# GFNet mixing and ReGLU on one core: last stores in multiples of 16 rows, the first input in four parts, slab loads queued behind the last slab store, and a longer lag in the first inverse transform

## The chip, the cores and the metric

The kernel runs on one core of a Trainium2 chip. The metric is the device time of one execution in microseconds (us), as the median of several executions. Executions that lie more than 1.5% above the fastest of the same kernel would be set aside as slow. A profile is one execution recorded by the hardware profiler. Its span is about 2 us shorter than the device time (967.1 against 969.6 us before), because the device time includes a little that lies outside the recorded span.

The engines are PE (matrix multiply), ACT (ScalarE), DVE (VectorE), POOL (GpSimd) and SP (used here only to issue DMAs). SP, ACT and POOL each have an in-order instruction stream, and each can issue DMAs from it. In a timeline, "SPq" or "ACTq" marks a stretch in which that stream was issuing DMAs.

## The reference

```python
# x: [8, 3008, 256], filters: [1505, 256], w_gate and w_val: [256, 1536], w_out: [1536, 256]
X = np.fft.rfft(x, axis=1)
y = np.fft.irfft(X * (filt_r + 1j * filt_i)[None], n=3008, axis=1)
t = y.reshape(24064, 256)
out = (np.maximum(t @ w_gate, 0.0) * (t @ w_val)) @ w_out
```

The kernel computes the Fourier transforms as matrix products over 3008 = 94 x 32. Stage A multiplies by a 94-point table (`psA`), stage B does the 32-point part, the filter and its inverse (`psX`, then `tt` and `uu`, then `psD`), and stage C finishes the inverse (`psY`). The feed-forward part then works on 47 blocks of 512 tokens (`psV`, `psG`, `psO`). Batches 1 to 7 of the transform are slipped in between the blocks. Only batch 0 has to be transformed before the first block can start, and only the last block's output has to be stored after the last matmul. These two ends are all that the change touches.

## The kernel before

Batch 0 goes through this chain: x from HBM into `XF`; 16 items of stage A, each a matmul into `psA` and a copy on ACT into `asb`; after every fourth item a store of `asb` to `Abuf` (a "slab store"); four "slab loads" of `Abuf` into `at`, in another layout; stage B; and so on. Stage B cannot start before all four slabs are in `at`.

```python
def load_at(b, c):                     # one slab: 32 x 24 runs of 512 bytes
    nc.sync.dma_start(ats[b][c:c + 125:4], _ap(Abuf[b], c * NROW * NC2 * D, [[D, 32], [4 * NC2 * D, NG], [1, D]]))

# in items_a, item j of slab c (cut)
nc.tensor.matmul(psA[0:NROW], WA[:, :NROW], XF[...][:, o:o + 512], start=True, stop=True)
nc.scalar.copy(dst, psA[0:NROW])
if j == 3:
    nc.sync.dma_start(_ap(Abuf[b], ...), st["asb"])

# in items_b: fwd(g) makes psX, tt (DVE) and uu (DVE, or for six g of batch 0 GpSimd) and appends to `held`;
# inv() takes the oldest of `held`, makes psD from tt and uu, copies it to dsb
for g in range(0, NG, 2):
    def both(g=g):
        fwd(g)
        if amid:
            amid(g // 2)
        if len(held) > 2:              # the lag
            inv()
    yield both
yield inv
yield inv

# the start (cut)
load_x(0, nc.sync, ((0, 0, 2 * q), (0, 2 * q, 4 * q), WHOLE[1]))
nc.sync.dma_start(tabs, ...)           # tables
hold_gpsimd(XF[0][:, 4 * q - 8:])      # GpSimd issues the filter loads only when this part of x is there
load_filters()
for i, f in enumerate(items_a(0)):
    f()
    if 9 <= i < 15:
        make_back(0, i - 9)            # psI: inverse tables, made from F2
    else:
        warm(1, 256)
    if i % 4 == 3 and i > 3:
        load_at(0, i // 4 - 1)
load_at(0, 3)
...
nc.sync.dma_start(gate, ats[0][0:32, NG - 1, 0:8])   # reads `at`: makes SP wait for the slabs
load_x(1, nc.sync, WHOLE)                            # x of batch 1
def amid(i):                           # inside stage B of batch 0:
    if i < 9:
        warm(1, 128)
    else:
        next(early)()                  # from the tenth step on, stage A of batch 1
```

The output is stored as follows. `runs` cuts 128 tokens into runs of at most 94 rows of 1 KB each, which lie 32 rows apart in the output.

```python
# in o_part; t is the quarter of the block, last the last block (cut)
nc.scalar.copy(osb[:, t0 % 2:t % 2 + 1], psO[:, t0 % 2:t % 2 + 1])
for tt in range(t0, t + 1):
    for i, (o, b, n2, n1, w) in enumerate(runs(blk * W + tt * 128, 128)):
        eng = nc.sync
        if last:
            eng = nc.gpsimd if t in (1, 2) else (nc.sync, nc.scalar)[i % 2]
        eng.dma_start(_ap(out, (b * S + n1 * N2 + n2) * D, [[N2 * D, w], [1, D]]), osb[o:o + w, tt % 2])
```

## Time and profile before

The median was 969.61 us (969.28 to 969.72 in 3 runs). Marks read from the trace split the span of 967.1 us into three parts:

| part | from, to (us) | length (us) |
|---|---|---|
| start: to the first psV matmul | 0, 60.83 | 60.83 |
| middle: first psV matmul to the end of the last matmul | 60.83, 958.10 | 897.28 |
| tail: from there to the span's end | 958.10, 967.1 | 8.96 |

The page of the kernel before gives each engine's busy time with its share of the span and its instruction count, and the shares of the chain of waits that ended last. PE is the bound, and only the two ends leave it idle for long.

```profile
PE 940.9 (97%) x5926; PEld 564.1 (58%) x6036; DVE 546.5 (57%) x823; ACT 527.4 (55%) x945; POOL 45.2 (5%) x81
...
PE 93%; DVE 2%; ACT 1%; issue 1%; DMA 1%; POOL 1%; SPq 0%; POOLq 0%; DVEq 0%; ACTq 0%
```

The stretches view of the tail before has these columns: the stretch and its length, then busy time and instruction count of PE, PEld, DVE, ACT and POOL, then the granted PE clock, the DMA engines' busy share and GB/s. From 962 us on, no compute engine has anything left, and the DMA engines are 12% and then 6% busy. Of 16 engines, 12% is two and 6% is one.

```profile
958.00:960.00 2.00, 0.10 (x1) 0.00 (x0) 0.00 (x0) 0.37 (x1) 0.76 (x2) 1.00 0.38 93
960.00:962.00 2.00, 0.00 (x0) 0.00 (x0) 0.00 (x0) 0.00 (x0) 0.00 (x0) 0.89 0.34 109
962.00:964.00 2.00, 0.00 (x0) 0.00 (x0) 0.00 (x0) 0.00 (x0) 0.00 (x0) 0.50 0.12 43
964.00:966.00 2.00, 0.00 (x0) 0.00 (x0) 0.00 (x0) 0.00 (x0) 0.00 (x0) 0.50 0.06 19
```

The timeline of ACT in the tail before gives start, length, engine, line, operation and count, and in brackets the idle time before it and what ended that. The last copies run at 956.83 and 958.14, right behind PE, and the last store is issued at 958.54. The landing records of that 94-row store show it complete at 965.62.

```profile
954.61 0.60 ACTq L406 DMA_DIRECT2D out_dram<-osb  x1
955.52 0.37 ACT L400 COPY osb<-psO 128x256 f32<-128x256 f32 x1 [0.94 <-PE psO L395]
956.83 0.37 ACT L400 COPY osb<-psO 128x256 f32<-128x256 f32 x1 [0.94 <-PE psO L395]
958.14 0.37 ACT L400 COPY osb<-psO 128x256 f32<-128x256 f32 x1 [0.94 <-DMA out_dram<-osb]
958.54 0.25 ACTq L406 DMA_DIRECT2D out_dram<-osb  x1
```

In the start, these are three of the waits of PE before 62 us (what waited, for what, us in total, times, the longest). The 4.4 us before psX are labelled "issue", but they end with the last slab load: the SP timeline below shows the read of `at` by `gate` passing at 35.02, and psX starts at 35.05.

```profile
PE psX L295 <- issue: 4.4, 1, 4.4
...
PE psD L315 <- POOL uu L302: 1.9, 4, 0.7
PE psI L189 <- DVE F L179: 1.0, 1, 1.0
```

The timeline of SP in the start before shows slab stores (`Abuf<-asb`) and slab loads (`at<-Abuf`) taking turns. A load waits for the landing of its own slab's store, and the last store, issued at 26.03, landed at 31.1.

```profile
21.59 0.31 SPq L268 DMA_DIRECT2D Abuf<-asb  x1
22.62 0.60 SPq L282 DMA_DIRECT2D at<-Abuf  x1
26.03 0.30 SPq L268 DMA_DIRECT2D Abuf<-asb  x1
28.16 3.56 SPq L282 DMA_DIRECT2D at<-Abuf  x2
35.02 0.31 SPq L459 DMA_DIRECT2D gate<-at  x1
```

### The profile page before, as it was taken

What the parts mean: (1) busy time and instruction counts of PE and PEld (TensorE: products, weight loads), DVE (VectorE), ACT (ScalarE), POOL (GpSimd) and SP (SyncE); (2) the same over time, 40 slices, a digit from 0 to 9 for tenths busy, and PEclk for the clock granted to TensorE, in tenths of its full rate; (3) what the DMA queues carried; (4) which work ended last, traced back from release to release, by engine and by line L of the source; (5) the groups of instructions that cost most, each with busy time, mean ns of one, the idle gap of its engine ahead of it and who ended that gap; (6) DMA issues with size and microseconds to landing.
All of it is one profiled execution on the core that took longest, in us unless ns stands there. A gap on an engine that the chain in (4) does not pass through costs nothing.

```text
span 967.1 us, 16199 instructions
## 1 busy us (share of the span) xinstructions
PE 940.9 (97%) x5926; PEld 564.1 (58%) x6036; DVE 546.5 (57%) x823; ACT 527.4 (55%) x945; POOL 45.2 (5%) x81
## 2 busy tenths in 40 slices
PE   8799999999999999999999999999999999999996
PEld 3446665466654666556665566655666556666664
DVE  3737855368543785437754377534775348655552
ACT  3665555555555555555555555555555555555552
POOL 4311000010000100001000010000100000000001
PEclk9899999999999999999999999999999999999998
DMA  9898151362523524135242352523524231241111
GB/s 248 247 242 250 61 127 30 101 209 65 119 57 83 205 81 112 49 101 191 77 115 55 104 197 55 115 70 109 174 64 113 69 110 41 82 99 34 33 33 45
DMA packets 94070, 105.64 MB, mean 109 GB/s; under 512 B 7724, under 2 KB 84929, under 8 KB 92298
## 3 DMA queue, kind: packets, MB, share of 16 engines
q1 hardware_dynamic: 87374, 81.44, 30.6%
q0 software_dynamic: 6432, 22.98, 8.1%
q8 instruction: 47, 0.77, 0.3%
q14 instruction: 33, 0.27, 0.1%
q10 hardware_dynamic: 184, 0.18, 0.1%
HBM read 58.67 MB, written 49.81 MB: 112 GB/s over the span
## 4 chain that ended last, share of the span: by engine, by line
PE 93%; DVE 2%; ACT 1%; issue 1%; DMA 1%; POOL 1%; SPq 0%; POOLq 0%; DVEq 0%; ACTq 0%
PE psO L395 25%; PE psG L376 25%; PE psV L376 23%; PE psA L263 10%; PE psY L360 2%; PE psD L315 2%; PE psX L295 2%; PE psD L314 2%; DMA tabs<-dft_tab 1%; DVE prod L381 1%; ACT vsb L379 1%; PE psJ L416 0%; POOL uu L302 0%; SPq L166 0%; ACT Fti L227 0%
## 5 line engine op out<-in xcount | busy, mean ns | idle before, releaser
L381 DVE SCALAR_TENSOR_TENSOR prod<-psG,vsb 128x512 bf16<-128x512 f32 x564 | 389.6, 691 | 368.0 <-ACT vsb L379 358.6
L379 ACT CAST vsb<-psV 128x512 bf16<-128x512 f32 x564 | 331.2, 587 | 212.1 <-PE psV L376 118.8
L395 PE MATMUL psO<-WoT,prod 128*128 128x256 bf16 x2256 | 336.5, 273 | 1.3
L376 PE MATMUL psG<-yT,WgT 128*128 128x512 bf16 x1096 | 328.5, 379 | 3.7
L376 PE MATMUL psV<-yT,WvT 128*128 128x512 bf16 x1051 | 319.2, 379 | 1.5 <-ACT yT L365 0.4
L395 PEld LDWEIGHTS <-prod 128*128 128x128 bf16 x2256 | 220.7, 98 | 143.4
L376 PEld LDWEIGHTS <-WgT 128*128 128x128 bf16 x1128 | 110.0, 98 | 134.0 <-issue 0.8
L376 PEld LDWEIGHTS <-WvT 128*128 128x128 bf16 x1128 | 104.2, 98 | 59.6 <-issue 49.5
L266 ACT CAST asb<-psA 96x512 bf16<-96x512 f32 x128 | 74.4, 581 | 109.3 <-PE psA L263 106.9
L263 PE MATMUL psA<-XF,WA 128*96 128x512 f32 x256 | 130.0, 593 | 0.9 <-DMA XF<-in_x_dram 0.9
L317 ACT CAST dsb<-psD 128x512 bf16<-128x512 f32 x96 | 56.2, 586 | 52.6 <-PE psD L315 50.6
L400 ACT COPY osb<-psO 128x512 f32<-128x512 f32 (+1 forms) x96 | 55.3, 577 | 29.3 <-PE psO L395 26.9
L298 DVE TENSOR_TENSOR tt<-psX,Ftr 128x512 bf16<-128x512 f32 x96 | 65.3, 681 | 4.5 <-PE psX L295 4.5
L304 DVE TENSOR_TENSOR uu<-psX,Fti 128x512 bf16<-128x512 f32 x90 | 61.2, 680 | 0.0
L315 PE MATMUL psD<-uu,I2u 128*128 128x256 bf16 x192 | 47.6, 275 | 1.9 <-POOL uu L302 1.9
L314 PE MATMUL psD<-tt,I2t 128*128 128x256 bf16 x192 | 48.1, 277 | 0.0
L360 PEld LDWEIGHTS <-dC 96*128 96x128 bf16 x604 | 34.6, 97 | 13.3 <-issue 10.8
L367 DVE CAST yT<-psY 128x512 bf16<-128x512 f32 x47 | 32.1, 683 | 17.5 <-PE psY L360 17.5
L295 PE MATMUL psX<-at,F 128*128 128x256 bf16 x192 | 37.6, 280 | 4.4 <-issue 4.4
L263 PEld LDWEIGHTS psA<-XF,WA 128*96 128x96 f32 x256 | 34.9, 163 | 8.8 <-ACT asb L266 3.6
L365 ACT CAST yT<-psY 128x512 bf16<-128x512 f32 x47 | 27.5, 585 | 19.6 <-PE psY L360 19.5
L360 PE MATMUL psY<-M,dC 96*128 96x94 bf16 (+18 forms) x604 | 37.7, 199 | 0.0
(52 smaller groups left out, 161.5 us busy)
## 6 DMA issues: line engine op xcount, KB each, us to landing
XF<-in_x_dram POOLq DMA_DIRECT2D x34, 512.0 KB, 6.6
Abuf<-asb SPq DMA_DIRECT2D x32, 384.0 KB
at<-Abuf SPq DMA_DIRECT2D x32, 384.0 KB
dC<-Dbuf SPq DMA_DIRECT2D x64, 192.0 KB
Dbuf<-dsb SPq DMA_DIRECT2D x31, 384.0 KB
out_dram<-osb SPq DMA_DIRECT2D x70, 94.0 KB
XF<-in_x_dram SPq DMA_DIRECT2D x9, 512.0 KB
XF<-in_x_dram SPq DMA_DIRECT2D x6, 256.0 KB
```

The costliest lines, as they stand in the source:

```text
L263: nc.tensor.matmul(psA[0:NROW], WA[:, :NROW], XF[c * NC2 // NX2][:, o:o + 512], start=True, stop=True)
L266: nc.scalar.copy(dst, psA[0:NROW])
L295: nc.tensor.matmul(psX[:, i], F2[:, g + i, :], at[:, g + i, :], start=True, stop=True)
L298: nc.vector.tensor_tensor(tt, psX, Ftr[:, g:g + 2, :], op=ALU.mult)
L304: nc.vector.tensor_tensor(uu, psX, Fti[:, g:g + 2, :], op=ALU.mult)
L314: nc.tensor.matmul(psD[:, i], I2t[:, g + i, :], tt[:, i], start=True, stop=False)
L315: nc.tensor.matmul(psD[:, i], I2u[:, g + i, :], uu[:, i], start=False, stop=True)
L360: nc.tensor.matmul(psY[:, o:o + w], dCs[b, n2 // 4][:, n2 % 4, h * 128:(h + 1) * 128], M1[:, n1:n1 + w], start=True, stop=True)
L376: nc.tensor.matmul(pt[:, :W], w[:, h, ft * 128:(ft + 1) * 128], yt[:, h, :], start=(h == 0), stop=(h == 1))
L379: nc.scalar.copy(vsb, psV[:, :W])
L381: nc.vector.scalar_tensor_tensor(prod, in0=psG[:, :W], scalar=0.0, in1=vsb, op0=ALU.max, op1=ALU.mult)
L395: nc.tensor.matmul(psO[:, t % 2], prods[ft][:, t * 128:(t + 1) * 128], WoT[:, ft, :], start=(ft == 0), stop=(ft == NFT - 1))
```

## The change

It has four parts:

1. The last block's stores are cut into a multiple of 16 rows and a rest. They alternate between SP and ACT, and GpSimd issues none.
2. x of batch 0 comes in four parts, with the tables ahead of the last part, and the filter loads start after the first quarter of x rather than the second.
3. The first slab load stands behind the third slab store, and the other three stand behind the fourth.
4. In stage B of batch 0 the inverse runs three steps behind the forward part, not two.

Two small things go with part 2: one warm-up matmul fewer, and psI starts one item of stage A later (`i >= 10` for `9 <= i < 15`).

```diff
--- before.py
+++ after.py
@@ -286,6 +286,7 @@
 
         held = []
         st = {}
+        lag = 2 if b else 3
         cuts = (0, 6, 12, 18, 24) if b else (0, 6, 12, 18, 22, 24)
 
         def fwd(g):
@@ -324,11 +325,11 @@
                 fwd(g)
                 if amid:
                     amid(g // 2)
-                if len(held) > 2:
+                if len(held) > lag:
                     inv()
             yield both
-        yield inv
-        yield inv
+        for _ in range(lag):
+            yield inv
 
     dCs = {}
 
@@ -400,11 +401,14 @@
             nc.scalar.copy(osb[:, t0 % 2:t % 2 + 1], psO[:, t0 % 2:t % 2 + 1])
             for tt in range(t0, t + 1):
                 for i, (o, b, n2, n1, w) in enumerate(runs(blk * W + tt * 128, 128)):
-                    eng = nc.sync
-                    if last:
-                        eng = nc.gpsimd if t in (1, 2) else (nc.sync, nc.scalar)[i % 2]
-                    eng.dma_start(_ap(out, (b * S + n1 * N2 + n2) * D, [[N2 * D, w], [1, D]]),
-                                  osb[o:o + w, tt % 2])
+
+                    cut = w // 16 * 16 if last else 0
+                    for c0, c1 in ((0, cut), (cut, w)):
+                        if c0 < c1:
+                            eng = nc.scalar if last and (t + i) % 2 else nc.sync
+                            eng.dma_start(_ap(out, (b * S + (n1 + c0) * N2 + n2) * D,
+                                              [[N2 * D, c1 - c0], [1, D]]),
+                                          osb[o + c0:o + c1, tt % 2])
 
 
     junk = pro.tile([128, 512], BF16, tag="junk", bufs=1)
@@ -424,25 +428,27 @@
     nc.gpsimd.memset(XF[0][:, 3 * q:], 0.0)
     nc.vector.memset(XF[1][:, 0:2 * q], 0.0)
     nc.gpsimd.memset(XF[1][:, 2 * q:], 0.0)
-    load_x(0, nc.sync, ((0, 0, 2 * q), (0, 2 * q, 4 * q), WHOLE[1]))
+    load_x(0, nc.sync, ((0, 0, 2 * q), (0, 2 * q, 4 * q), (1, 0, 2 * q)))
     nc.sync.dma_start(tabs, nc.inline_tensor(tab_h, name="dft_tab").ap())
+    load_x(0, nc.sync, ((1, 2 * q, 4 * q),))
     for (src, dst) in FILT:
         nc.vector.memset(dst[64:128, NG - 2:, :], 0.0)
-    hold_gpsimd(XF[0][:, 4 * q - 8:])
+    hold_gpsimd(XF[0][:, 2 * q - 8:2 * q])
     load_filters()
     load_own_filters()
 
-    warm(12)
+    warm(11)
     place_forward()
     for i, f in enumerate(items_a(0)):
         f()
-        if 9 <= i < 15:
-            make_back(0, i - 9)
+        if i >= 10:
+            make_back(0, i - 10)
         else:
             warm(1, 256)
-        if i % 4 == 3 and i > 3:
-            load_at(0, i // 4 - 1)
-    load_at(0, 3)
+        if i == 11:
+            load_at(0, 0)
+    for c in range(1, 4):
+        load_at(0, c)
     for half in range(2):
         for a in range(2):
             place_filter(0, a, half, nc.vector.tensor_copy)
```

## The prediction

> **What bounds the kernel.** By the chain of waits PE holds 93% of the span, and the page has PE busy 97%; between about 62 and 958 us the second half (psV, psG, psO) runs back to back on PE. The change touches nothing there. It can only move the first 62 us and the 9 us after PE's last matmul (958.1).
>
> **Tail.** PE stops at 958.1, the last osb copy ends at 958.5, the span ends at 967.1. The DMA view of the last 9 us shows why: the ACT queue still moves about 40 GB/s until 965.3. That is the last 94-row store; the trace's landing records show only two late increments (964.7 and 965.6), so it ran on two engines, 47 rows each, about 0.12 us a row. The Trainium skill (DMA: Bandwidth & Descriptors, "Why a DMA increments its semaphore by 16 and not by 1") says that the engine count is the largest number up to 16 that divides the rows; 94 gives 2, and this trace agrees. The change cuts it into 80 (16 engines, 5 rows each) and 14 (14 engines, 1 row each). A 16-row store of this trace, issued at 953.5, landed at 954.9. GpSimd's tail stores (5.1 to 5.8 us to landing) go too. Cost: more issues, about 0.3 us each; ACT's copies are at most 0.2 us late. I expect the last landing near 960.6 and 1.5 us of closing as now: about 4.8 us gained.
>
> **Start, part A.** Tables landed at 17.2 and PE waited 1.0 us for F (waits view); that wait goes. But the filter loads now start at about 8.3 instead of 10.9 and slow the last x quarter: in 17 to 20 us the GpSimd queue took 125% of the engines' time and the SP queue 11%. So PE may wait 0 to 3 us at item 12.
>
> **Slab loads.** What really ends the start is the last at<-Abuf load: SP waited for it until 35.0, PE's psX began at 35.05 after 4.4 us idle. The DMA engines were busy until 29, then lost about 3 us in 29 to 35 waiting for landings (first slab issued 18.9, landed 27.3; last store issued 26.0, landed 31.2). Now the last store goes ahead of three slab loads, which fill its landing time. I expect the last slab at about 33: 2 us gained.
>
> **Longer lag in B.** PE waited 1.9 us for GpSimd's uu (4 waits); these should nearly go. But B then meets the next batch's x: its first half landed at 45.3, psA of that batch ran at 45.7, only 0.4 us later. This load is issued only once the last slab is in, and the Dbuf stores queue behind it. So the lag alone gains about nothing; it covers a later DVE start. The whole start gains what the slab gains.
>
> **Sum.** 969.6 - 4.8 - 2.0 = 962.8 us, range 960.9 to 965.2. Faster by over 2%: 0.005; within 2%: 0.99; slower: 0.005.
>
> **Signs.** Right: last matmul near 956.1; from it to the span's end 4 to 4.5 us, not 9; psX starts near 33; waits of psD for GpSimd under 0.5 us; a new wait of PE psA for XF of 0.5 to 2 us before 45 us; psY of block 0 near 57.5. Wrong: psA waits over 3 us at item 12, or psX not before 34.5; a last landing after 962.
>
> **What would upset it.** Filters starving the last x quarter longer than the slab order gains; slab loads slower together than alone; the batch-1 x arriving sooner than 10.3 us after the last slab, when the lag would pay a further 1 to 1.5 us; ACT's extra issues delaying its copies.

## The result, and the profile after

In one job the kernel after took 965.90 us (965.78 to 966.31, 4 runs) and the kernel before 969.44 us (968.89 to 969.72, 4 runs), so 3.5 us were gained. A ratio here is the ratio of fast runs, which is not quite the ratio of the quoted medians. This one is 0.9965, with a 95% interval of 0.9948 to 0.9982. The predicted 962.8 us and the range of 960.9 to 965.2 both lie below the measurement.

The marks of the two first profiles, and of a second profile of each kernel (`before_again`, `after_again`), are:

| mark (us) | before | before again | after | after again |
|---|---|---|---|---|
| last stage A item of batch 0 | 24.34 | 24.25 | 22.68 | 22.77 |
| first psX | 35.05 | 35.73 | 34.54 | 34.24 |
| first psA of batch 1 | 45.71 | 46.39 | 44.70 | 44.63 |
| first psY | 59.62 | 60.29 | 59.08 | 59.02 |
| first psV | 60.83 | 61.50 | 60.51 | 60.23 |
| end of the last matmul | 958.10 | 958.66 | 957.79 | 957.38 |
| last osb copy, after the last matmul | 0.41 | 0.41 | 2.82 | 2.93 |
| last landing, after the last matmul | 7.52 | 7.02 | 5.36 | 5.13 |
| tail | 8.96 | 8.46 | 6.39 | 6.16 |

The middle took 897.15 to 897.38 us in every profile, so everything happens at the ends. The tail gave 2.6 us in the first profiles and 2.4 in the means of both, where 4.8 had been predicted. Of these 2.4, 0.4 us is the closing, from the last landing to the span's end: it went from 1.4 us in both profiles of before to 1.0 in both of after, which nobody had predicted and no run explains. The start gave 0.3 us at psV in the first profiles. Because the start varies from one execution to the next, more profiles are needed: the eight that have exactly the start of the kernel after (these two and six of the experiments) mean 59.89 at psV, against 61.17 for the two of before, a gain of 1.3 where 2.0 had been predicted. The tail's 2.4 and this 1.3 make 3.7, close to the 3.5 and 3.0 us that the two timings of the unchanged kernel after gave.

The page of the kernel after differs little: PE is just as busy in a span 2.9 us shorter, and POOL has five instructions fewer, as many as the stores that it no longer issues.

```profile
PE 940.5 (98%) x5925; PEld 564.4 (59%) x6035; DVE 546.6 (57%) x823; ACT 527.6 (55%) x945; POOL 43.1 (4%) x76
...
PE 93%; DMA 4%; DVE 1%; ACT 1%; issue 1%; POOL 0%; ACTq 0%; SPq 0%; POOLq 0%
```

In the stretches of the tail after, the long drain of one or two engines is gone, but there are now copies of ACT in both of the first stretches, though PE stopped at 957.79.

```profile
958.00:960.00 2.00, 0.00 (x0) 0.00 (x0) 0.00 (x0) 0.37 (x1) 0.00 (x0) 1.00 0.24 68
960.00:962.00 2.00, 0.00 (x0) 0.00 (x0) 0.00 (x0) 0.37 (x1) 0.00 (x0) 0.91 0.39 102
962.00:964.00 2.00, 0.00 (x0) 0.00 (x0) 0.00 (x0) 0.00 (x0) 0.00 (x0) 0.50 0.16 48
```

The timeline of ACT in the tail after says why. Three DMA issues hold ACT from 955.86 to 958.80, and the copy behind them waits 3.08 us, ended by "DMA" where before it was ended by PE. The last copy starts at 960.23, 2.4 us after the last matmul ended.

```profile
953.90 0.37 ACT L401 COPY osb<-psO 128x256 f32<-128x256 f32 x1 [0.72 <-PE psO L396]
954.30 0.98 ACTq L409 DMA_DIRECT2D out_dram<-osb  x2
955.45 0.37 ACT L401 COPY osb<-psO 128x256 f32<-128x256 f32 x1 [1.18 <-DMA out_dram<-osb]
955.86 2.94 ACTq L409 DMA_DIRECT2D out_dram<-osb  x3
958.91 0.37 ACT L401 COPY osb<-psO 128x256 f32<-128x256 f32 x1 [3.08 <-DMA out_dram<-osb]
959.31 0.82 ACTq L409 DMA_DIRECT2D out_dram<-osb  x2
960.23 0.37 ACT L401 COPY osb<-psO 128x256 f32<-128x256 f32 x1 [0.95 <-DMA out_dram<-osb]
```

What holds an issue is told by the trace's DMA records, listed here for the stores around that stretch. Each DMA reports its completion on a semaphore. The program's DMAs from SP and ACT use eight of them in turn, so each shares its semaphore with the one eight before it, and the last column is the landing of that earlier one.

```
kernel after
issued   by   rows  landed   semaphore  its last user landed
953.56   SP   94    957.41   102        941.05      (block before the last, uncut)
953.88   SP   18    957.59   104        943.48      (block before the last, uncut)
954.27   SP   76    958.48   106        948.27      (block before the last, uncut)
954.30   ACT  80    958.79   105        943.67
...
957.43   SP   10    959.99   102        957.41
957.61   ACT  16    960.17   104        957.59
958.50   ACT  10    960.36   106        958.48
958.87   SP   80    960.54   105        958.79
...
961.29   SP   80    962.99   105        960.54
961.66   SP   14    963.15   115        961.07
```

Four issues in a row, at 957.43, 957.61, 958.50 and 958.87, came 0.02 to 0.08 us after the landing of the store eight before. The instruction records say the same: each of the four, or the semaphore instruction just before it, names that shared semaphore as what it waits for. The wait is thus part of the program as it was built. Those earlier stores were slow because the change leaves the stores of the block before the last uncut: the 94-row store took 3.9 us, and the 80-row store issued 0.7 us behind it took 4.5, where a free 80-row store takes 1.7 (the 80-row line at 961.29). The Trainium skill (DMA: Bandwidth & Descriptors, "Anatomy of one DMA — SWDGE (gpsimd) path") says that the DMA engines do not wait on semaphores: "any semaphore wait happens on the issuing sequencer before dispatch". This trace agrees for SP and ACT: ACT's stream stood still for 2.94 us with three issues in it.

In the start, the waits of PE after show the wait of psI for F gone, 1.9 us for POOL down to 0.6, and the wait for the slabs longer, since stage A ends 1.7 us earlier.

```profile
PE psX L296 <- DMA at<-Abuf: 5.4, 1, 5.4
...
PE psA L263 <- ACT xs L302: 1.3, 1, 1.3
...
PE psD L316 <- POOL uu L303: 0.6, 2, 0.3
```

The timeline of SP in the start after shows the new slab order. The last store is issued at 24.37 rather than 26.03, with three slab loads behind it, but these three need 6.39 us to be issued.

```profile
19.93 0.30 SPq L268 DMA_DIRECT2D Abuf<-asb  x1
20.33 0.65 SPq L282 DMA_DIRECT2D at<-Abuf  x1
24.37 0.31 SPq L268 DMA_DIRECT2D Abuf<-asb  x1
24.78 6.39 SPq L282 DMA_DIRECT2D at<-Abuf  x3
34.49 0.31 SPq L465 DMA_DIRECT2D gate<-at  x1
```

From the landing records of the first profiles and three experiments:

```
                             before          after           s_filtlate      s_allslab
last slab store, issue-land  26.03 - 31.1    24.37 - 30.6    24.69 - 29.6    24.46 - 28.2
last slab load, issue-land   31.14 - 35.0    30.60 - 34.4    29.62 - 33.5    28.22 - 34.7
last large filter load landed   26.3            28.6            27.1            26.7
```

### The profile page after: what moved, and what is told of

Same layout as the page of the kernel before. It is cut to its first block, busy times and chain, and to the rows that moved or that the text cites. A ratio compares the mean times of both kernels' runs of the same rounds, so it can differ in the third digit from the quotient of the medians.

```text
span 964.2 us, 16212 instructions
## 1 busy us (share of the span) xinstructions
PE 940.5 (98%) x5925; PEld 564.4 (59%) x6035; DVE 546.6 (57%) x823; ACT 527.6 (55%) x945; POOL 43.1 (4%) x76
## 4 chain that ended last, share of the span: by engine, by line
PE 93%; DMA 4%; DVE 1%; ACT 1%; issue 1%; POOL 0%; ACTq 0%; SPq 0%; POOLq 0%
PE psG L377 25%; PE psO L396 25%; PE psV L377 24%; PE psA L263 10%; PE psY L361 2%; PE psX L296 2%; PE psD L315 2%; PE psD L316 2%; DMA Dbuf<-dsb 1%; DMA Abuf<-asb 1%; DVE prod L382 1%; DMA dC<-Dbuf 1%; ACT vsb L380 0%; DMA XF<-in_x_dram 0%; DMA out_dram<-osb 0%
## 5 line engine op out<-in xcount | busy, mean ns | idle before, releaser
L368 DVE CAST yT<-psY 128x512 bf16<-128x512 f32 x47 | 32.1, 684 | 18.1 <-PE psY L361 18.1
L366 ACT CAST yT<-psY 128x512 bf16<-128x512 f32 x47 | 27.5, 586 | 19.7 <-PE psY L361 19.5
```

## The experiments

Each experiment is the kernel after with one edit, unless said otherwise. All gave correct results. "Job's before" is the median of the kernel before in the same job. The list of marks is in one table, after the experiments on the start.

### The tail

The theory: the late copies on ACT are caused by issues that wait for a completion semaphore, because stores of the block before the last are long. The rivals: ACT simply has too many issues to make; or the stores are now limited by SP's issues or by the DMA engines, so that the copies do not matter.

**t_cutprev** also cuts the second half of the stores of the block before the last.

```diff
-                    cut = w // 16 * 16 if last else 0
+                    cut = w // 16 * 16 if last or blk == NB - 2 and tt >= 2 else 0
```

> The changed kernel, with the stores of the block before the last (its last two 128-row tiles) cut into multiples of 16 rows as well. Theory 1 (the eight completion semaphores are reused in turn, and the last block's short stores wait for the uncut stores of the block before, the 94-row one above all): no copy of psO in the last block waits for a store any more, the last copy starts within 0.3 us of the last matmul's end, from the last matmul to the span's end 4.3 us instead of 6.4, time near 963.9. Theory 2 (the number of issues is the cost, about 0.3 us each): five more issues, so 6.4 us or more, time 966 or more.

It took 965.65 us (job's before 969.05, ratio 0.9962, 0.9946 to 0.9979), and the tail was 6.07 us rather than 6.39 and 6.16. The copies came 1.23 us after the last matmul ended rather than 2.8 to 2.9, so the semaphore waits shrank as the theory says, but the tail hardly did. Both theories missed: the first had promised a last copy within 0.3 us and a tail of 4.3, the second a tail of 6.4 or more. The 80-row and 14-row stores of the last quarter were still issued only at 960.36 and 960.72, 2.9 and 3.3 us after the last matmul, as SP now has 17 of the 26 late stores to issue.

**t_dve** puts the last block's copies on DVE, so that they no longer stand in ACT's stream.

```diff
-            nc.scalar.copy(osb[:, t0 % 2:t % 2 + 1], psO[:, t0 % 2:t % 2 + 1])
+            (nc.vector.tensor_copy if last else nc.scalar.copy)(osb[:, t0 % 2:t % 2 + 1], psO[:, t0 % 2:t % 2 + 1])
```

> The changed kernel, with the last block's psO copies on VectorE, so that ScalarE only issues. Theory 1 (semaphores held by the uncut stores): the copies run at PE's pace, but the stores still come late because they wait for landings at about 957.4 to 958.8; from the last matmul to the end 5.0 to 5.8 us, time near 965.2. Theory 3 (the harm is only that copies stand behind issues in ScalarE's queue): 4.3 us, time near 963.9.

It took 964.93 us (job's before 969.05, ratio 0.9957, 0.9942 to 0.9972). The copies were on time (0.46 us after the last matmul), and yet the tail was 6.46 us. So late copies alone are not what the tail waits for either, and again both expectations were missed (5.0 to 5.8, or 4.3). The run also settles a rival. A copy has to wait for the stores that used its `osb` buffer before, and there are five buffers; here the copies ran on time with the same five, so the buffers were not what made them late.

**t_both** has both edits.

> The cut of the run t_cutprev and the copies on VectorE of t_dve together, without dealing out in turn (17 of 26 late stores on the SyncE queue). Each alone left 6.1 and 6.5 us after the last matmul. If long stores and copies behind issues were all: 4.2 to 4.6 us. If the SyncE queue's run of 17 issues, about 0.45 us each, is the third limit: 5.0 to 5.8 us.

It took 965.30 us (job's before 968.52, ratio 0.9967, 0.9953 to 0.9981), with a tail of 6.02 us, above both expected ranges but nearer to the one that blamed SP's 17 issues. The timeline of DVE shows the last copy on time, and the timeline of SP shows what is left.

```profile
956.82 0.42 DVE L401 COPY osb<-psO 128x256 f32<-128x256 f32 x1 [0.88 <-PE psO L396]
```

```profile
952.19 8.25 SPq L409 DMA_DIRECT2D out_dram<-osb  x17
```

SP issues 17 stores from 952.19 to 960.44, about 0.49 us each (8.25 / 17, waits included). The last 80-row store was issued at 959.66, though its data had been copied at 957.24 and its semaphore had been free since 958.19. It then landed as fast as any, in 1.7 us.

**t_best** works on all three limits: copies on DVE, late stores of both blocks cut only where they would otherwise get fewer than 8 engines (so 21 late stores, not 26), and dealt in turn to ACT and SP.

```diff
-            nc.scalar.copy(osb[:, t0 % 2:t % 2 + 1], psO[:, t0 % 2:t % 2 + 1])
+            (nc.vector.tensor_copy if last else nc.scalar.copy)(osb[:, t0 % 2:t % 2 + 1], psO[:, t0 % 2:t % 2 + 1])
-                    cut = w // 16 * 16 if last else 0
+                    late = last or blk == NB - 2 and tt >= 2
+                    few = max(k for k in range(1, 17) if w % k == 0) < 8
+                    cut = w // 16 * 16 if late and few else 0
-                            eng = nc.scalar if last and (t + i) % 2 else nc.sync
+                            ost["n"] = ost.get("n", 0) + late
+                            eng = nc.scalar if late and ost["n"] % 2 else nc.sync
```

> The changed kernel with three changes of the tail: psO copies of the last block on VectorE; late stores cut only where they would run on fewer than 8 engines, in the last block and in the last two tiles of the block before (21 late stores, not 22 or 26, and none of 94 or 76 rows); late stores dealt out in turn to the two queues. If long stores and one queue's run of issues together make the tail: each late store lands within 2.5 us of its issue, last landing within 2.7 us of the last matmul, from the last matmul to the end 4.2 to 4.7 us, time near 963.6. If the issues alone (21, as many as now): over 5.8 us.

It took 962.93 us (job's before 969.07, ratio 0.9938, 0.9921 to 0.9954), with a tail of 4.24 us and the last landing 3.14 us after the last matmul (within 2.7 had been expected). Two early issues, at 953.90 and 955.71, still came 0.02 us after the landing of the store eight before, but none after the last matmul did. The stretches view of its tail shows all work over before 960 us, with PE ending at 956.82.

```profile
956.00:958.00 2.00, 0.82 (x8) 0.49 (x5) 0.42 (x1) 0.00 (x0) 0.00 (x0) 1.00 0.26 72
958.00:960.00 2.00, 0.00 (x0) 0.00 (x0) 0.00 (x0) 0.00 (x0) 0.00 (x0) 0.86 0.34 100
960.00:962.00 2.00, 0.00 (x0) 0.00 (x0) 0.00 (x0) 0.00 (x0) 0.00 (x0) 0.50 0.00 0
```

**t_best_uncut** is t_best without the cuts in the block before the last.

```diff
-                    cut = w // 16 * 16 if late and few else 0
+                    cut = w // 16 * 16 if last and few else 0
```

> t_best with the stores of the block before the last uncut again (one of 94 and one of 76 rows), still dealt out in turn, copies on VectorE. Theory 1 (the long stores hold two engines and their semaphores, and the last block's stores queue behind them): from the last matmul to the end 5.2 to 6.2 us, several stores issued within 0.05 us of the landing of the store eight before, time near 964.4. Theory 2 (what t_best gained came from dealing out and from fewer issues on one queue): 4.2 to 4.6 us, time near 963.0.

It took 964.50 us (job's before 968.5, ratio 0.9958, 0.9945 to 0.9972), with a tail of 5.72 us, as the first theory had it (5.2 to 6.2). Six issues again came within 0.01 to 0.08 us of the landing of the store eight before, for instance at 956.51, 956.89 and 957.30 after landings at 956.45, 956.87 and 957.29.

**t_best_act** is t_best with the copies left on ACT.

```diff
-            (nc.vector.tensor_copy if last else nc.scalar.copy)(osb[:, t0 % 2:t % 2 + 1], psO[:, t0 % 2:t % 2 + 1])
+            nc.scalar.copy(osb[:, t0 % 2:t % 2 + 1], psO[:, t0 % 2:t % 2 + 1])
```

> t_best with the psO copies back on ScalarE, which also issues half of the late stores. Theory 3 (a copy stands behind the issues ahead of it in ScalarE's queue, about 0.3 to 0.6 us each): the last copy ends 0.9 to 2 us after the last matmul instead of 0.46, from the last matmul to the end 4.8 to 5.8 us, time 963.6 to 964.5. If the copies were late only through long stores: 4.2 to 4.5 us.

It took 965.06 us (job's before 968.5, ratio 0.9964, 0.9949 to 0.998), with copies 2.61 us late and a tail of 5.92 us. Both are worse than expected (0.9 to 2 us, and 4.8 to 5.8), in the direction that the theory of the copies gave.

What follows for the tail: three limits stood side by side, namely issues waiting for old long stores, copies behind issues in ACT's stream, and too many issues on SP. Taking away the first, the second, or those two together left the tail between 6.0 and 6.5 us. Easing all three gave 4.24, and putting back either of the first two gave 5.7 to 5.9. The third was not put back by itself: t_both differs from t_best in its dealing and in its count of stores at once, so the split of that step between the two is open. A gap of 0.4 us in t_both's row of SP issues, at 957.25, has no cause that I found.

### The start

The theory: the last slab store lands late because it is queued behind the first slab load and the filters. The last slab load, which cannot be issued before that landing, then takes another 3.8 us to land. The rivals: the earlier filters alone hold it up; or the longer lag in B costs or gains something; or the load order is at fault.

**s_filtlate** holds the filters on the second quarter of x again, as before.

```diff
-    hold_gpsimd(XF[0][:, 2 * q - 8:2 * q])
+    hold_gpsimd(XF[0][:, 4 * q - 8:])
```

> The changed kernel with the filter loads held as before, until the second quarter of x is in. Seen so far in four kernels with the changed start: psX begins at 33.5 to 34.5 (before: 35.05). Theory Y (the queue of slab traffic and filters is the same work whenever the filters start, so their earlier start bought nothing): psX within 33.4 to 34.6. Theory Z (the earlier filters took the turn of the slab stores and the first slab load, and cost what the slab order gained): psX near 32.8 or earlier, filters landed by 26.5.

It took 965.64 us (job's before 969.07, ratio 0.9964, 0.9949 to 0.9979). The first psX came at 33.62, inside the 33.5 to 34.5 of the eight profiles with the start of the kernel after, and the time is theirs too. The timing of the filters is not what decides.

**s_allslab** issues all four slab loads after the fourth store.

```diff
-        if i == 11:
-            load_at(0, 0)
-    for c in range(1, 4):
+    for c in range(4):
```

> The changed kernel with the first slab load as well behind the last slab store. The last slab load cannot be issued before the last store has landed (29.5 to 30.6, 5 to 6 us after its issue), and takes 3.8 us. Theory Q (that store is late because it stands behind the first slab load in the queue): it lands near 27.5 to 28.5, psX begins near 32.5 to 33. Theory D (it is late because the engines are full with filters until 27 to 28): it still lands at 29 or later, psX at 34 or later since the first load now comes later.

It took 966.14 us (job's before 969.07, ratio 0.997, 0.9955 to 0.9985). Now the last store landed at 28.2, the earliest of all, which confirms that the first slab load ahead of it had been in its way. But four loads then followed one another, landing at 29.5, 32.1, 33.4 and 34.7, and psX started at 34.79. What the store gained, the loads behind it took back. Of the two theories, the first was right for the store (27.5 to 28.5) and wrong for psX (32.5 to 33).

**s_slab** is the kernel before with the new slab order alone.

```diff
-        if i % 4 == 3 and i > 3:
-            load_at(0, i // 4 - 1)
-    load_at(0, 3)
+        if i == 11:
+            load_at(0, 0)
+    for c in range(1, 4):
+        load_at(0, c)
```

> The kernel before with the slab order alone (first slab load after the third slab store, the others after the fourth); x, tables, filters, lag and stores as before. Six runs with the whole changed start had psX at 33.5 to 34.5, 1.0 us earlier than before in the mean. Theory Y (the slab traffic and the filters fill the engines until about 28 in any order, then one slab load per 1.3 us): the last A item stays at 24.3, psX at 34.0 to 35.3, so 0 to 1 us. Prediction on record (slab order is what gains): psX near 33.

It took 967.65 us (job's before 968.5, ratio 0.999, 0.9977 to 1.0004). Stage A ended at 24.20 as before, but psX started at 34.37 and psV at 60.15. That is 1.0 us earlier than the mean of the two profiles of the kernel before, most of what the whole new start gives (1.3). The timing agrees in size (0.85 us between the medians), though its interval includes no gain at all.

**s_lag2** puts the lag back to 2.

```diff
-        lag = 2 if b else 3
+        lag = 2
```

> The changed kernel with the lag of the first B stage back at 2. Theory X (B ends with the landing of the next batch's x): psD's waits for GpSimd return to about 1.9 us, but psA of batch 1 starts at 44.7 within 0.3 us and psY of block 0 at 59.1 to 59.6, time 965.9 within 0.5. Rival (the lag gave what the start gained): psA of batch 1 at 45.3 or later, everything after it 0.5 to 1 us later, time 966.4 to 966.9.

It took 965.36 us (job's before 969.05, ratio 0.9961, 0.9946 to 0.9976). PE waited 2.2 us for GpSimd's uu rather than 0.6, and next to nothing came of it: psA of batch 1 began 10.46 us after psX, against 10.16 and 10.39 with the lag of 3. The time is that of the kernel after.

**s_nogate** removes the read of `at` that holds the x load of batch 1 until the slabs have landed. The output was correct without it; the line only keeps the load's traffic out of the slabs' way.

```diff
-    nc.sync.dma_start(gate, ats[0][0:32, NG - 1, 0:8])
```

> The changed kernel without the small store that holds back the load of batch 1's x until the last slab has landed; x then only queues behind the slab load. Theory X: x's first half lands 2 to 3 us earlier (near 42), psA of batch 1 starts near 43.3 instead of 44.7, psY of block 0 near 58.2, time 1.0 to 1.5 us less (964.6). Rival (psA there waits for ScalarE's copies or for psD, not for x): psA stays at 44.5 or later, time 965.9.

It took 963.61 us (job's before 969.05, ratio 0.9943, 0.9928 to 0.9957). The first half of x of batch 1 landed at 38.6 rather than 44.5, psA of batch 1 began 8.70 us after psX, and psX itself was not late (33.53). The direction was expected, but x came about 3 us earlier and the time 1 us lower than that (near 42, and 964.6).

**s_nogate_lag2** has that edit and the lag of 2.

> The changed kernel without the small store that holds back batch 1's x, and with the lag of the first B stage at 2. With x early (38.6 in the run without that store) B is limited by its own work: from the first psX to psA of batch 1 9.5 to 10 us instead of 8.7, psY of block 0 about 1 us later, time about 1 us more (964.6). If the lag is worth nothing there either: 8.7 us and 963.6.

It took 965.71 us (job's before 969.07, ratio 0.9966, 0.9951 to 0.998), and psA of batch 1 began 10.66 us after psX, where 9.5 to 10 and 964.6 us had been expected. x was early here too (38.4). The waits of PE for GpSimd's uu in s_nogate, then in s_nogate_lag2, each followed by the first psA of batch 1 in the timeline of PE:

```profile
PE psD L316 <- POOL uu L303: 0.7, 2, 0.5
...
42.22 1.02 PE L263 MATMUL psA<-XF,WA 128*96 128x512 f32 x2
```

```profile
PE psD L316 <- POOL uu L303: 2.8, 4, 1.6
...
44.61 1.02 PE L263 MATMUL psA<-XF,WA 128*96 128x512 f32 x2
```

So the lag is worth 2.0 us (10.66 - 8.70) once x is there in time, and 2.1 us in the timings (963.61 against 965.71, each close to the same median of before). With x late it is worth next to nothing. This also corrects a line of the profile after: it puts the 1.3 us wait of psA down to "ACT xs", but with x early that wait is absent at the same lag, so it was x that was waited for. x landed at 44.45, and psA ran at 44.70. In all eleven profiles that have the start of the kernel after with the gate line (s_filtlate, s_allslab and s_lag2 included), psA of batch 1 ran 0.24 to 0.25 us after that landing.

| kernel | last A item | first psX | first psA of batch 1, after psX | first psV | last matmul | last copy, last landing after it | tail |
|---|---|---|---|---|---|---|---|
| t_cutprev | 22.98 | 34.38 | 10.29 | 60.27 | 957.42 | 1.23, 4.79 | 6.07 |
| t_dve | 22.62 | 33.67 | 10.29 | 59.56 | 956.71 | 0.46, 5.42 | 6.46 |
| t_both | 22.63 | 33.62 | 10.20 | 59.50 | 956.78 | 0.46, 4.74 | 6.02 |
| t_best | 22.70 | 33.68 | 10.39 | 59.66 | 956.82 | 0.46, 3.14 | 4.24 |
| t_best_uncut | 22.67 | 33.52 | 10.36 | 59.72 | 957.11 | 0.46, 4.44 | 5.72 |
| t_best_act | 22.82 | 33.89 | 10.22 | 59.70 | 956.86 | 2.61, 4.83 | 5.92 |
| s_filtlate | 23.00 | 33.62 | 10.27 | 59.49 | 956.74 | 2.96, 5.20 | 6.23 |
| s_allslab | 22.76 | 34.79 | 10.38 | 60.77 | 957.93 | 2.94, 5.19 | 6.22 |
| s_slab | 24.20 | 34.37 | 10.66 | 60.15 | 957.33 | 0.41, 6.98 | 8.41 |
| s_lag2 | 22.73 | 33.86 | 10.46 | 59.48 | 956.66 | 3.09, 5.22 | 6.25 |
| s_nogate | 22.82 | 33.53 | 8.70 | 57.77 | 954.93 | 2.90, 5.25 | 6.34 |
| s_nogate_lag2 | 22.98 | 33.95 | 10.66 | 59.72 | 956.87 | 2.94, 5.31 | 6.40 |
| best | 23.07 | 34.59 | 8.69 | 58.83 | 955.98 | 0.46, 3.35 | 4.58 |
| best_again | 23.18 | 33.76 | 8.69 | 58.00 | 955.34 | 0.46, 3.23 | 4.45 |

### The repeats, and the version that beats both

**before_again** and **after_again** are the two kernels unchanged, to see how far the start varies.

> The kernel before, unchanged, for a second profile. If the start of one and the same kernel repeats, psX begins at 35.05 within 0.2 us; if it varies from execution to execution as much as the changed start did over ten kernels (33.5 to 34.8), anywhere from 34.3 to 35.6. From the last matmul to the end 8.9 us within 0.3.

It took 969.11 us against 968.52 for the same kernel in the same job (ratio 1.0007, 0.9988 to 1.0025), as one kernel against itself should. Its psX came at 35.73, 0.7 us later than in the first profile and just outside the widest range expected; its tail, 8.46 us, was shorter than expected by more than the 0.3 allowed. One profile of a kernel is thus good to about 0.7 us in the start and 0.5 us in the tail.

> The changed kernel, unchanged, for a second profile. Its first profile had psX at 34.54, other kernels with the same code up to there 33.5 to 34.6. If the start varies by execution: anywhere in 33.4 to 34.8; if it belongs to the built kernel: 34.54 within 0.2. From the last matmul to the end 6.4 us within 0.2. Time 965.9 within 0.5.

It took 965.48 us (job's before 968.52, ratio 0.9969, 0.9954 to 0.9984), with psX at 34.24 and a tail of 6.16 us, both nearly where expected.

The last slab store shows where such differences come from. In all 18 profiles but one, psX started 3.7 to 4.1 us after that store had landed (the exception is s_allslab, with four loads behind it: 6.6). In four of the five profiles where it landed latest, the last of its 16 engines reported 1.3 to 1.7 us after the fifteenth (29.3 and 30.6 in the kernel after, 30.3 and 32.0 in before_again); in the others it was 0.1 to 1.2 us (29.1 and 29.6 in s_filtlate, 29.3 and 29.8 in best_again). Why one engine straggles in some executions stays open.

**best** is t_best without the gate line, and **best_again** is the same kernel once more.

> The tail of t_best together with the start of s_nogate on the changed kernel. The two ends are 897 us apart and nothing between them has moved in any run, so they should add: 963.6 (s_nogate) less 2.1 (tail 6.34 to 4.24) gives 961.5, or 962.9 (t_best) less 2.0 to 2.5 gives 960.4 to 960.9; span near 959.2. If they do not add: above 962.5.

It took 962.34 us (job's before 968.5, ratio 0.9934, 0.9922 to 0.9947).

> The kernel of the run best, unchanged. Its profile had psX at 34.59 (late among its kind) and 4.58 us after the last matmul. If the start varies by execution, psX may now lie near 33.7, and the time in rounds is 961.5 to 962.4; if it belongs to the built kernel: 34.6 within 0.2, and 962.3.

It took 962.43 us (job's before 968.52, ratio 0.9935, 0.9922 to 0.9947). This version beats both kernels: it is 6.1 us faster than the kernel before, and 3.0 us faster than the kernel after that was timed in the same job as best_again (965.48). It is 0.8 to 0.9 us slower than the upper end of the 960.4 to 961.5 us that adding the two gains had promised. Part of that is seen: the tails were 4.58 and 4.45 us rather than 4.24, and psX in `best` came at 34.59, about 1 us later than in the two experiments that were added. In best_again psX was early (33.76) and the profiled span, 959.8 us, was close to the sum; but the median of its five runs was not. The rest is not settled.

## Why the prediction was right or wrong

It was right that only the two ends could move, that the gain would be below 2%, and that the middle would stay (897.28 us in both first profiles). It was too optimistic by 3.1 us, of which the tail is the larger part.

**Tail: the cause was right, the step "ACT's copies are at most 0.2 us late ... I expect the last landing near 960.6" failed.** The 94-row store did run on two engines. The Trainium skill (DMA: Bandwidth & Descriptors, "Why a DMA increments its semaphore by 16 and not by 1") gives the rule from which 94 rows get 2 engines and 80 get 16. The traces agree: 7.1 us from issue to landing for the last 94-row store of the kernel before, with two late increments, and 1.7 and 1.5 us for the 80 and the 14 rows of the kernel after. But the copies came 2.8 us after the last matmul, not 0.6, and the last landing 5.4 us after it, not 2.5. The prediction priced the added issues at about 0.3 us each and had listed "ACT's extra issues delaying its copies" among what would upset it. It did not look at what an issue can wait for: the landing of the store eight before it, which in this place is a long, uncut store of the previous block. Nor did it count SP's issues. With all three limits eased, t_best had its last landing 3.14 us after the last matmul and a tail of 4.24 us, which is within the predicted 4 to 4.5: that tail can be had, but the change alone did not reach it. The match is partly luck, since the landing was 0.6 us later than predicted and the closing 0.4 us shorter (1.1, not 1.5). The prediction's "GpSimd's tail stores ... go too" was not tested by itself. SP's own stores of the same stretch before, 52 rows issued at 954.92 and 42 rows at 955.34, took 4.6 and 5.4 us to land, so the 5.1 to 5.8 us of GpSimd's don't show that GpSimd made them slow.

**Start, part A: right.** The wait of 1.0 us for F went, stage A ended 1.7 us earlier, and there was no wait for x at item 12 (predicted 0 to 3 us). Whether the earlier tables or the later psI removed the wait was not separated. The 0.7 us wait for XF that the waits view after lists is that of the first item, in place of one of 0.9 us before. (The 125% and 11% in the prediction are the view of 17.3 to 20 us; for 17 to 20 it says 115.3% and 17.5%.)

**Slab loads: the mechanism was right, the term "2 us" was mis-sized.** In the first profiles the store went out 1.7 us earlier and landed 0.5 us earlier (30.6 against 31.1); in the means it landed 1.6 us earlier (29.97 in the eight profiles against 31.57 in the two). s_slab, in one profile, splits this: the new order alone brought the store, issued at 25.89, to land at 30.28, and issuing it 1.5 us earlier as well won only another 0.3 us. It still stood behind the first slab load (s_allslab: 28.2 without it); that the filters held it up too is argued, not shown. The last load could go only after that landing, and took 3.8 us as before, so a slab at 33 would have needed the store in by about 29.2. "Last slab at about 33" became 34.4 in the first profile, and psX came on the average of eight profiles at 33.94, against 35.39 in two of before: 1.4 us. psV gained 1.3. The reading "or psX not before 34.5" that the prediction had named as a sign against it came true in the first profile, at 34.54; in the others psX was earlier.

**Longer lag: right, and its condition too.** Alone it gained next to nothing (s_lag2: psA of batch 1 ran 10.46 us after psX, against 10.16 to 10.39). The prediction said that it would pay 1 to 1.5 us if x of batch 1 came sooner, and with x sooner it paid 2.0 to 2.1. The sign "waits of psD for GpSimd under 0.5 us" was nearly met (0.6), and the predicted wait of psA for x of 0.5 to 2 us is there (1.3), under the wrong name.

**Sum.** The prediction took 4.8 + 2.0. The runs showed about 2.4 + 1.3. Its other signs of being right failed with these two terms: the last matmul ended at 957.79 rather than near 956.1, psY began at 59.08 rather than near 57.5, and the last landing came at 963.15, after the 962 that it had named as a sign of being wrong.

## What to carry to other kernels

When several limits stand side by side at the end of a kernel (old stores that hold a reused semaphore, copies behind issues in one in-order stream, too many issues on one queue), removing one of them can move almost nothing, as here, so list them all and check each issue time against what it could have waited for. Do not put a DMA issue that can wait ahead of a copy that the end of the kernel needs in the same stream, and treat the block before the last as part of the tail. Before crediting an earlier load or store, ask what it queues behind and what its landing releases: here the same lag was worth nothing with the next input late and 2 us with it early.

## What the Trainium skill lacked or had wrong

- DMA: Bandwidth & Descriptors, "Anatomy of one DMA — SWDGE (gpsimd) path", says that semaphore waits happen on the issuing sequencer. None of the pages that I read adds that a program as built may make an issue wait for the completion semaphore that it shares with an earlier DMA. Here eight semaphores served SP and ACT in turn, and issues came 0.02 to 0.08 us after the landing of the store eight before; ACT lost about 2 us to it in one place (2.94 us for three issues that take 0.28 to 0.33 us each).
- The same page, "Issuing engines are not separate DMA queues", says that issuing from several engines saves only the sequencer's time, "which is usually small relative to the DMA itself". For a run of small stores it adds up: in t_both 17 issues held SP for 8.25 us, waits included, while a store of 80 rows took 1.7 us to land.
- The same page, "Why a DMA increments its semaphore by 16 and not by 1", says that the engines finish independently. It gives no number for how far apart: for the last slab store of batch 0, the last of 16 came from 0.1 to 1.7 us after the fifteenth in 18 profiles. The landing records do not name the engine, and the cause is open.
